# Block sums of w2 made in DRAM scratch, and the seventh block product of the second MLP product made wide

## The chip, the cores and the metric

The kernel runs on one core of one Trainium2 chip. The core has a matrix engine (TensorE, PE in the profile; PEld is its weight load), a vector engine (VectorE, DVE), a scalar engine (ScalarE, ACT), a general engine (GpSimd, POOL), a queue engine (SyncE, SP) and sixteen DMA engines that all queues share. Each engine works through its own instructions in their order, and semaphores tie them together. The metric is the device time of one execution in microseconds; lower is better.

## The reference

One transformer block on `x` of shape (1, 2048, 512), all in float32. First a linear attention, added to `x`:

```python
h = x + A(layernorm(x))
# A: qkv = x @ wqkv, 32 heads of 16
#    phi(q) = [softmax(q w_phi), softmax(-q w_phi)], phi(k) likewise
#    o = phi(q) (phi(k)^T v) / (phi(q) sum(phi(k)) + 1e-6);  A = o @ wo
```

Then an MLP across the 2048 tokens (not the channels), with F = 1792:

```python
g = layernorm(layernorm(h))                       # (S, D)
u = gelu(einsum("sd,sf->df", g, w1) + b1)         # first product,  w1: 2048 x 1792
y = einsum("df,fs->ds", u, w2) + b2               # second product, w2: 1792 x 2048
out = h + y^T
```

## The kernel before

**Precision by parts.** Each float32 matrix is split into a rounded part and a remainder. A product of two such matrices is three matmuls: high by high, high by low, low by high. In the code the first part is made by ACT (a copy into a rounded type) and the second by DVE or POOL (a subtraction), mostly in the helper `split`.

**First stage.** Weights are centred and folded, keys and values are projected for 16 tiles of 128 tokens, and their softmax sums are gathered. PE's order there is written by hand (`PASSES`); the order of the other engines and of SP came from a planner that simulates a timeline.

**Attention stage.** From `ms.enter_context(tc.manual_schedule(...))` on, the order of all five engines is as written. A loop runs `it` over 0 to 17. In iteration `it` SP loads a tile of `x` (`s_x`, the tile `h`), may load a tile pair of w1 for the first part of the first product (`turn`, `fill_load`, `stream`, line 691), and stores the finished `h` of the tile before (`s_h`, line 642). ACT rounds the loaded w1 in the same iteration (`his`, line 677), and DVE later forms its remainder (`flush`, line 684). PE multiplies the numerators (`s_num`), transposes (`s_tr`), does query projections, the output projection `po` (`s_wo`, lines 71 to 73; it needs `oh` from ACT and `ol` from DVE, line 625), and the part of the first product that is already possible (`fill`).

**First and second product.** The rest is a list of 96 steps (`STEPS`): kinds `v u u v v` of the first product, eight steps each, and from step 40 on the second product, eight blocks of 256 output columns (`sp`) with seven steps (`p`) each. In the `u` and `y` steps a 2 x 2 grid of 128-blocks of the weight is multiplied in the manner of Strassen and Winograd with seven block products instead of eight. Each needs one of seven combinations of the four weight blocks and one of seven of the data. The seven weight operands lie in one tile `wraw` of seven places: places 1 to 4 are loaded, and places 0, 5 and 6, and in the second product place 1 as well, are sums. In a `y` step these are four DVE additions, done at once for four steps (`w_sums`, lines 793, 794, 795, 797). In the `u` steps one of the sums is made by an adding DMA of POOL instead (`add_raw`, line 783).

A block product of the second product comes in two shapes. `narrow` (line 951) is three matmuls of 256 columns into one place. `wide` (lines 958 and 960) is one matmul of the rounded weight with the high and low data side by side, 512 columns, and one of 256 columns for the weight's remainder; it fills two places of a bank, and the second has to be added at the end. In the seven full blocks the products P2, P3, P4 and P5 are wide, and P1, P6 and P7 are narrow. The last column block (`last_step`) has all products narrow.

At the end of a column block ACT and DVE read the six banks out and form four output tiles, and POOL adds them to `out` in DRAM with adding DMAs (`store`, line 1001).

**Loads and buffers.** `load_raw(g)` loads the weight of steps 2g and 2g + 1, one transfer of 256 KB each (and one of 64 KB more in `u` steps), into one of two blocks of four steps. It is issued eight steps ahead; SP waits until DVE has read the old contents. `prepare` makes the parts of a step (`w_parts`, lines 66 and 67) two steps ahead in the first product and five in the second.

Of the kernel before, what the change touches and what calls it, by code (L numbers as in the profile page):

```python
# [9 lines left out]
F32 = mybir.dt.float32  # L10
F32R = mybir.dt.float32r
AF = mybir.ActivationFunctionType
ALU = mybir.AluOpType
# [4 lines left out]
P = 128  # L18
# [5 lines left out]
NPR = 2 * NG  # L24
Q_EARLY = 6

PASSES = [(s[0], int(s[1:] or 0)) for s in
          "k5 v f k6 v q k7 q v k8 v q v q k9 k10 v k11 q k12 v k13 v q k14 v".split()]
PKS = 8
SUMS = 8  # L30
Q_TURNS = ((0, 1), (0, 1), (0, 1), (0, 1), (0,), (1,), (0,), (1,))
# [11 lines left out]
def block_kernel(ctx: ExitStack, tc: tile.TileContext, x, xT, wT, phic, wo, w1, b1, w2, b2,  # L43
# [2 lines left out]

    cst = ctx.enter_context(tc.tile_pool(name="cst", bufs=1))
    big = ctx.enter_context(tc.tile_pool(name="big", bufs=NT + 2))

    ident = cst.tile([P, P], F32, name="ident")  # L50
    mask = cst.tile([P, 64], F32, name="mask")
# [55 lines left out]
    X, XH, EQ, PK, VS, SQ, PS, W = {}, {}, {}, {}, {}, {}, {}, {}  # L107

    def load_x(t):
        raw = kk.tile([P, KD, P], F32, name="xraw", bufs=3)  # L110
# [7 lines left out]
    def split_x(t, raw, alone=False):  # L118
# [4 lines left out]
        else:  # L123
            split(X[t][:, 0], X[t][:, 1], raw, nc.gpsimd)

    def stats_x(t):
        junk = kk.tile([P, D], F32, name="sqj", bufs=1)
        st = kk.tile([P, 2], F32, name="st")
        nc.scalar.activation(junk, XH[t], AF.Copy, scale=-1.0 / D, accum_out=st[:, 0:1])
        nc.scalar.activation(junk, XH[t], AF.Square, bias=st[:, 0:1], accum_out=st[:, 1:2])  # L130
        ve = kk.tile([P, 1], F32, name="ve")
        nc.vector.tensor_scalar(ve, st[:, 1:2], 1.0 / D, EPS, op0=ALU.mult, op1=ALU.add)
        nc.gpsimd.tensor_tensor(r1[:, t:t + 1], ve, mhalf[:, :1], op=ALU.pow)

    def proj(t, wh, wl, pool, name, by_part=False, halves=1):
        o = pool.tile([P, D], F32, name=name, tag=name)
# [24 lines left out]
    def logit_ops(src, e, pool):  # L161

        v = src.rearrange("p (j h d) -> p j h d", h=2, d=DH)
        ev = signs(e)
        mx = wk.tile([P, NPR, 2], F32, name="mx")
        mn = wk.tile([P, NPR, 2], F32, name="mn")

        def shift():
            nc.vector.tensor_sub(ev[:, :, 0], v, mx.unsqueeze(3).to_broadcast([P, NPR, 2, DH]))
            if pool:  # L170
                MN.append((ev, mx, mn))
            else:
                nc.vector.tensor_sub(ev[:, :, 1], mn.unsqueeze(3).to_broadcast([P, NPR, 2, DH]), v)  # L173

        return [lambda: nc.vector.tensor_reduce(mx, v, axis=AX.X, op=ALU.max),
                lambda: nc.vector.tensor_reduce(mn, v, axis=AX.X, op=ALU.min),
                shift]

    def negate():

# [9 lines left out]
    def run(*lists):  # L190
        for op in turns(*lists):
            op()

    def exps(t, e):
        nc.scalar.activation(e, e, AF.Exp, scale=r1[:, t:t + 1])  # L195

    def heads(e):
        return e.rearrange("p g (a d) -> p (g a) d", d=DH)

    def k_ops(t, o):  # L200
        PK[t] = kk.tile([P, NG, P], F32, name="pk", bufs=PKS)
        run(logit_ops(o, PK[t], False))

    def k_logits(t):
        k_ops(t, proj(t, wkh, wkl, ps_k, "pk_ps"))
        exps(t, PK[t])

    def v_out(t, o):
        VS[t] = kk.tile([P, D], F32, name="vs", bufs=5)
# [2 lines left out]
    def v_proj(t):  # L212
        v_out(t, proj(t, wvh, wvl, ps_v, "pv"))

    def k_norm(t, z=True):
        sk = wk.tile([P, 2 * H], F32, name="sk", bufs=2)
        nc.vector.reduce_sum(sk, heads(PK[t]), axis=AX.X)
        nc.vector.reciprocal(sk, sk)  # L218
        nc.gpsimd.tensor_mul(heads(PK[t]), heads(PK[t]), sk.unsqueeze(2).to_broadcast([P, 2 * H, DH]))  # L219
        if z and t == 0:  # L220
            nc.gpsimd.tensor_copy(zacc, PK[t])
        elif z:
            nc.gpsimd.tensor_add(zacc, zacc, PK[t])  # L223

    def kv(t):

# [54 lines left out]
    with tc.tile_pool(name="prep", bufs=1) as prep:  # L281
# [77 lines left out]
        with tc.manual_schedule(engines={ET.PE, ET.DVE, ET.Activation, ET.Pool}):  # L359
# [61 lines left out]
            lo_w(0)  # L421
            lo_w(1)
            center(3, False)
        stats_x(3)
        exps(3, PK[3])
        load_h(4)
        stats_x(4)
        k_ops(4, k4)
        exps(4, PK[4])
        v_out(2, v2)  # L430

        def fold_rest():
            for c in range(2, 4):
                fold(c, ps_q, "pu")
                hi_w(c)
                lo_w(c)

        def k_step(t):

            if t + 2 < NT:  # L440
                raw = load_x(t + 2)
                load_h(t + 2)
            if t > 4:
                k_logits(t)
            k_norm(t - 1)
            if t + 2 < NT:
                split_x(t + 2, raw)
                stats_x(t + 2)

        def q_step(_):  # L450
            q_mm()
            run(q_logits(0))
            q_exp(0)
            run(q_sums(0))


        with tc.manual_schedule(engines={ET.PE}):
            k_step(3)
            k_step(4)
            for name, n in PASSES:  # L460
                {"k": k_step, "v": lambda _: v_kv(), "q": q_step, "f": lambda _: fold_rest()}[name](n)

    ms = ExitStack()
    ms.enter_context(tc.manual_schedule(engines={ET.PE, ET.DVE, ET.Activation, ET.Pool, ET.SP}))
# [203 lines left out]
    w1v = w1.rearrange("(k p) f -> p k f", p=P)  # L668
    w2v = w2.rearrange("(k p) s -> p k s", p=P)

    COMING, LATER = [], []

    def his():
# [85 lines left out]
    def load_raw(g):  # L759
        if 2 * g >= len(STEPS):  # L760
            return
        b = g // 2 % 2
        if b not in BLOCK:
            BLOCK[b] = cbb.tile([P, 4, 7, P], F32, name="wraw") if b else wqp.tile([P, 4, 7, P], F32, name="wraw", tag="wq")
        RAW[g] = BLOCK[b][:, g % 2 * 2:g % 2 * 2 + 2]
        for k in range(2):
            src, r, c = blocks(2 * g + k)
# [18 lines left out]
    def w_sums(g):  # L786

        if 2 * g >= len(STEPS) or STEPS[2 * g][0] == "v":
            return
        plain = STEPS[2 * g][0] == "y"  # L790
        raw = BLOCK[g // 2 % 2] if plain else RAW[g]
        if plain:
            nc.vector.tensor_add(raw[:, :, 0], raw[:, :, 3], raw[:, :, 1])
# [35 lines left out]
    for it in range(NT + 2):  # L829
        if it < NT:  # L830
            s_x(it)
        shifted = q["logits"] - len(MN)
        ql = q_logits(0)
        work = turn(it)
# [168 lines left out]
    def wide_step(n, sp, p):  # L1003
        t = 2 * sp
        if p == 0:
            b3, b2 = [new_bank((ps_f, ps_q)[sp % 2]) for _ in range(2)]
            BK[:] = [new_bank(ps_b) for _ in range(4)] + [b3, b2]
        b16, b7, b5, b4, b3, b2 = BK
        first, end = p == 0, p == NP - 1

        def x(m):
            return UB[p, m]

        def ws_(*products):
# [31 lines left out]
        add(e0, l5, u2)  # L1046
# [211 lines left out]
```

## Time and profile before

The median of three runs is 516.4 us (516.31 to 516.42). One execution was profiled:

| what | value |
|---|---|
| the profiled execution's own time | 516.23 us |
| its span, first to last instruction | 514.5 us |
| TensorE clock granted | 1.00 of full speed |
| PE busy | 509.4 us |
| DVE busy | 432.5 us |
| ACT busy | 300.7 us |
| POOL busy | 247.1 us |
| bytes moved by DMA | 61.76 MB |

The span and the time differ by what lies before the first and after the last instruction. The span falls into the first stage (to about 137 us), the attention stage (to about 264 us), the steps of the first product (to about 372 us) and the second product.

How to read the lines. A line of a group gives line, engine, operation, output <- inputs, shapes and count, then busy time and mean length of one in ns, then the idle time of the engine before these instructions and what ended it. A line of the timeline gives start and length in us and then the same. Matmuls are pipelined, so the length of one is longer than the distance between two starts; the distance tells what a matmul costs. A DMA line gives engine that issues, count, KB each and the median time from issue to landing.

### The profile page before, as it was taken

What the parts mean: (1) busy time and instruction counts of PE and PEld (TensorE: products, weight loads), DVE (VectorE), ACT (ScalarE), POOL (GpSimd) and SP (SyncE); (2) the same over time, 40 slices, a digit from 0 to 9 for tenths busy, and PEclk for the clock granted to TensorE, in tenths of its full rate; (3) what the DMA queues carried; (4) which work ended last, traced back from release to release, by engine and by line L of the source; (5) the groups of instructions that cost most, each with busy time, mean ns of one, the idle gap of its engine ahead of it and who ended that gap; (6) DMA issues with size and microseconds to landing.
All of it is one profiled execution on the core that took longest, in us unless ns stands there. A gap on an engine that the chain in (4) does not pass through costs nothing.

```text
span 514.5 us, 10292 instructions
## 1 busy us (share of the span) xinstructions
PE 509.4 (99%) x3954; PEld 439.7 (85%) x3954; DVE 432.5 (84%) x736; ACT 300.7 (58%) x530; POOL 247.1 (48%) x195
## 2 busy tenths in 40 slices
PE   9999999999999999999999999999999999999997
PEld 8888888888877777777788999988899999999997
DVE  6799889989887899699876878986789989968973
ACT  6999853526267878867675636555364434434530
POOL 3579997876999999975203330000002112211220
PEclk9999999999999999999999999999999999999999
DMA  8642301020113233443329784333425687668743
GB/s 306 218 143 84 103 22 42 1 77 8 43 62 103 81 104 126 147 160 126 103 79 256 152 194 120 103 103 102 143 63 126 162 194 172 128 152 192 168 63 71
DMA packets 52112, 61.76 MB, mean 120 GB/s; under 512 B 4704, under 2 KB 38752, under 8 KB 52064
## 3 DMA queue, kind: packets, MB, share of 16 engines
q1 hardware_dynamic: 45440, 52.43, 32.6%
q0 software_dynamic: 6336, 8.52, 12.1%
q8 instruction: 31, 0.51, 0.4%
q10 hardware_dynamic: 288, 0.17, 0.1%
q14 instruction: 17, 0.14, 0.1%
HBM read 49.96 MB, written 11.14 MB: 119 GB/s over the span
## 4 chain that ended last, share of the span: by engine, by line
PE 95%; DVE 2%; ACT 1%; issue 0%; DVEq 0%
PE py L951 22%; PE pu L71 10%; PE pu L72 9%; PE pu L73 9%; PE py L958 9%; PE py L960 4%; PE pk_ps L71 3%; PE pk_ps L72 3%; PE pk_ps L73 3%; PE pv L73 3%; PE pv L72 3%; PE pv L71 3%; PE po L71 3%; PE po L73 2%; PE po L72 2%; PE pn L616 2%
## 5 line engine op out<-in xcount | busy, mean ns | idle before, releaser
L66 ACT ACTIVATE wp<-wraw 128x896 fp32r<-128x896 f32 (+1 forms) x96 | 79.8, 869 | 83.4 <-DVE wraw L797 34.1
L67 DVE TENSOR_TENSOR wp<-wraw,wp 128x896 fp32r<-128x896 f32 (+1 forms) x96 | 92.3, 986 | 20.7 <-ACT wp L66 20.5
L1001 POOL DMA_DIRECT2D out<-u x28 | 24.5, 952 | 170.0 <-ACT u L1047 110.8
L951 PE MATMUL py<-cb,wp 128*128 128x256 f32 x582 | 79.8, 283 | 0.0
L951 PEld LDWEIGHTS py<-cb,wp 128*128 128x128 f32 x582 | 74.0, 191 | 0.0
L490 POOL TENSOR_TENSOR ez<-eq,zB 128x1024 f32<-128x1024 f32 x16 | 38.4, 2404 | 3.8 <-ACT zB L550 3.8
L71 PE MATMUL pu<-hs,wp 128*128 128x512 f32 x96 | 37.4, 389 | 0.0
L72 PE MATMUL pu<-hs,wp 128*128 128x512 f32 x96 | 37.4, 389 | 0.0
L73 PE MATMUL pu<-hs,wp 128*128 128x512 f32 x96 | 37.3, 389 | 0.0
L219 POOL TENSOR_TENSOR pk<-pk,sk 128x1024 f32<-128x1024 f32 x16 | 31.1, 1943 | 11.3 <-DVE sk L218 10.1
L958 PE MATMUL py<-cb,wp 128*128 128x512 f32 x126 | 36.1, 394 | 0.0
L514 POOL TENSOR_TENSOR eq<-eq,w 128x1024 f32<-128x1024 f32 x16 | 32.4, 2026 | 3.5 <-DVE w L511 3.5
L223 POOL TENSOR_TENSOR zacc<-zacc,pk 128x1024 f32<-128x1024 f32 x13 | 31.3, 2406 | 0.5
L783 POOL DMA_DIRECT2D wraw<-in_w x16 | 14.2, 970 | 31.7 <-DMA wraw<-in_w 21.3
L195 ACT ACTIVATE pk<-pk,r 128x1024 f32<-128x1024 f32 x16 | 18.4, 1148 | 15.0 <-DVE pk L173 14.4
L951 PE MATMUL py<-uf,wp 128*128 128x256 f32 x198 | 26.6, 283 | 0.0
L71 PE MATMUL pu<-wq,xs 128*128 128x512 f32 x64 | 26.1, 408 | 0.0
L71 PE MATMUL pu<-hs,whl 128*128 128x512 f32 x64 | 26.0, 406 | 0.0
L71 PE MATMUL po<-woh,oh 128*128 128x512 f32 x64 | 25.3, 395 | 0.1
L72 PE MATMUL pu<-wq,xs 128*128 128x512 f32 x64 | 25.0, 391 | 0.0
L72 PE MATMUL pu<-hs,whl 128*128 128x512 f32 x64 | 25.0, 390 | 0.0
L73 PE MATMUL po<-woh,ol 128*128 128x512 f32 x64 | 25.0, 390 | 0.0
(213 smaller groups left out, 1398.5 us busy)
## 6 DMA issues: line engine op xcount, KB each, us to landing
wraw<-in_w SPq DMA_DIRECT2D x112, 256.0 KB, 3.4
out<-u POOLq DMA_DIRECT2D x21, 256.0 KB, 5.2
xraw<-in_xT SPq DMA_DIRECT2D x16, 256.0 KB, 3.0
xh<-in_x SPq DMA_DIRECT2D x16, 256.0 KB, 2.6
h<-in_x SPq DMA_DIRECT2D x16, 256.0 KB, 2.8
out<-h SPq DMA_DIRECT2D x16, 256.0 KB, 2.0
wraw<-in_wT SPq DMA_DIRECT2D x12, 256.0 KB, 5.2
wraw<-in_w POOLq DMA_DIRECT2D x16, 128.0 KB, 3.9
```

What stands on the lines that cost most here:

```text
L66: nc.scalar.activation(hi, src, AF.Copy)
L67: lo_engine.tensor_sub(lo, src, hi)
L71: nc.tensor.matmul(o, ah, bh, start=first, stop=False)
L72: nc.tensor.matmul(o, ah, bl, start=False, stop=False)
L73: return nc.tensor.matmul(o, al, bh, start=False, stop=last).ins
L219: nc.gpsimd.tensor_mul(heads(PK[t]), heads(PK[t]), sk.unsqueeze(2).to_broadcast([P, 2 * H, DH]))
L223: nc.gpsimd.tensor_add(zacc, zacc, PK[t])
L490: nc.gpsimd.tensor_mul(EZ[t], EQ[t], zB)
L514: nc.gpsimd.tensor_mul(heads(EQ[t]), heads(EQ[t]), W[t].rearrange("p g c h -> p (g c h)").unsqueeze(2).to_broadcast([P, 2 * H, DH]))
L951: nc.tensor.matmul(o, w[:, m[0]], x[:, y], start=opens and i == 0, stop=closes and i == 2, skip_group_check=True)
L958: nc.tensor.matmul(o, wh_[:, m[0]], x(m[1]), start=first, stop=False, skip_group_check=True)
L1001: nc.gpsimd.dma_start(out[t * P:(t + 1) * P, k * HD:], flat(a), accum_op=ALU.add)
```

## The change

1. Scratch in DRAM. For each column block `sp` of w2 a scratch tensor `w2s` of 128 x 7 x 2 x 128 is kept. `copy_w2(sp)` fills it with two DRAM-to-DRAM transfers on SP's queue, in iterations 0 to 7 of the attention loop, directly behind the load of `h`. `add_w2(sp)` adds 128 x 7 x 256 of w2 to it with one adding transfer of POOL's queue; these stand at steps 18, 20, ..., 32 of the first product.
2. Loads. A `y` step now takes places 0 and 1 (both sums) from the scratch and places 2 and 3 to 4 from w2: three transfers instead of one.
3. DVE. The two additions that made places 0 and 1 are gone.
4. P7 is wide in the seven full column blocks. At their end one more ACT copy and one more DVE subtraction bring in the second place of its bank. In a block's first step P7 goes with P5 and P4 instead of before them; in its last step it comes after the narrow products.
5. The order of the first stage is now written out for all engines as a list of tokens (`FIRST`), one token for one operation on one tile.

```diff
+FIRST = """
+X5 H4 X6 a5 X7 b5 a6 b6 H5 X8 X9 s3 a7 S3 b7 a8 H6 X10 u3 b8 l4 r3 s4 m4 n2 k5 S4 o2 H7 X11 x4 y4 s5 N2 v3 u4
...
+    def copy_w2(sp):
+        W2S[sp] = dram.tile([P, NP, 2, P], F32, name=f"w2s{sp}")
+        src = w2v.rearrange("p (j i) s -> p j i s", i=2)
+        for k in range(2):
+            nc.sync.dma_start(W2S[sp][:, :, k], src[:, :, 1 - k, 2 * sp * P:2 * sp * P + P])
+
+    def add_w2(sp):
+        src = w2v.rearrange("p (j i) s -> p j i s", i=2)
+        nc.gpsimd.dma_start(W2S[sp].rearrange("p j k s -> p j (k s)"), src[:, :, 0, 2 * sp * P:2 * sp * P + 2 * P],
+                            accum_op=ALU.add)
...
+        with tc.manual_schedule(engines={ET.PE, ET.DVE, ET.Activation, ET.Pool, ET.SP}):
+            for token in FIRST.split():
+                DO[token[0]](int(token[1:]))
...
+            if kind == "y":
+                nc.sync.dma_start(RAW[g][:, k, 0:2], W2S[i][:, j])
+                nc.sync.dma_start(RAW[g][:, k, 2], src[:, r, c + P:c + 2 * P])
+                nc.sync.dma_start(RAW[g][:, k, 3:5].rearrange("p i s -> p (i s)"), src[:, r + 1, c:c + 2 * P])
+                continue
...
-        if plain:
-            nc.vector.tensor_add(raw[:, :, 0], raw[:, :, 3], raw[:, :, 1])
         nc.vector.tensor_add(raw[:, :, 5], raw[:, :, 0], raw[:, :, 2])
         nc.vector.tensor_add(raw[:, :, 6], raw[:, :, 4], raw[:, :, 5])
-        if plain:
-            nc.vector.tensor_add(raw[:, :, 1], raw[:, :, 1], raw[:, :, 2])
...
         if it < NT:
             s_x(it)
+        if 0 <= it - 0 < 0 + NT // 2:
+            copy_w2(it - 0)
...
-        w3, w2, w5, w4 = (b3, P3), (b2, P2), (b5, P5), (b4, P4)
+        w3, w2, w5, w4, w7 = (b3, P3), (b2, P2), (b5, P5), (b4, P4), (b7, P7)
         if first:
             ws_(w3, w2)
         elif not end:
-            ws_(w3, w2, w5, w4)
+            ws_(w3, w2, w5, w4, w7)
         narrow(b16[:, 0], n, P1, x(1), first, end)
         narrow(b16[:, 1], n, P6, x(5), False, end)
-        narrow(b7[:, 0], n, P7, x(0), first, end)
         if first:
-            ws_(w5, w4)
+            ws_(w7, w5, w4)
         if not end:
             return []
+        ws_(w7)
         ws_(w4, w5)
         ws_(w3, w2)
...
+        nc.scalar.activation(e0, b7[:, 1], AF.Copy)
         sub(u3, u2, b7[:, 0])
...
+        sub(u3, u3, e0)
...
+    for sp, n in ((0, 18), (1, 20), (2, 22), (3, 24), (4, 26), (5, 28), (6, 30), (7, 32)):
+        at(n, add_w2, sp)
```

More of the change, by code (lines that the diff above doesn't have):

```diff
@@ L124, in split_x, with stats_sum, stats_square, stats_var @@
             split(X[t][:, 0], X[t][:, 1], raw, nc.gpsimd)
-    def stats_x(t):
[L127 to L133, printed above, removed]
+    def stats_sum(t):
+        junk = kk.tile([P, D], F32, name="sqj", bufs=1)
+        ST[t] = kk.tile([P, 2], F32, name="st")
+        nc.scalar.activation(junk, XH[t], AF.Copy, scale=-1.0 / D, accum_out=ST[t][:, 0:1])
+    def stats_square(t):
+        junk = kk.tile([P, D], F32, name="sqj", bufs=1)
+        nc.scalar.activation(junk, XH[t], AF.Square, bias=ST[t][:, 0:1], accum_out=ST[t][:, 1:2])
+    def stats_var(t):
+        ST[t], st = kk.tile([P, 1], F32, name="ve"), ST[t]
+        nc.vector.tensor_scalar(ST[t], st[:, 1:2], 1.0 / D, EPS, op0=ALU.mult, op1=ALU.add)
+    def stats_rstd(t):
+        nc.gpsimd.tensor_tensor(r1[:, t:t + 1], ST[t], mhalf[:, :1], op=ALU.pow)
+    def stats_x(t):
+        for f in (stats_sum, stats_square, stats_var, stats_rstd):
+            f(t)
     def proj(t, wh, wl, pool, name, by_part=False, halves=1):
@@ L213, in v_proj, with norm_sum, norm_rec, norm_mul @@
         v_out(t, proj(t, wvh, wvl, ps_v, "pv"))
-    def k_norm(t, z=True):
[L216 to L223, printed above, removed]
+    def norm_sum(t):
+        SK[t] = wk.tile([P, 2 * H], F32, name="sk", bufs=2)
+        nc.vector.reduce_sum(SK[t], heads(PK[t]), axis=AX.X)
+    def norm_rec(t):
+        nc.vector.reciprocal(SK[t], SK[t])
+    def norm_mul(t):
+        nc.gpsimd.tensor_mul(heads(PK[t]), heads(PK[t]), SK[t].unsqueeze(2).to_broadcast([P, 2 * H, DH]))
+    def norm_z(t):
+        if t == 0:
+            nc.gpsimd.tensor_copy(zacc, PK[t])
+        else:
+            nc.gpsimd.tensor_add(zacc, zacc, PK[t])
+    def k_norm(t, z=True):
+        norm_sum(t)
+        norm_rec(t)
+        norm_mul(t)
+        if z:
+            norm_z(t)
     def kv(t):
@@ L423, in block_kernel @@
             center(3, False)
[L424 to L448, printed above, removed]
@@ L450, in q_step, with k_mm @@
-        def q_step(_):
-            q_mm()
[L452 to L461, printed above, removed]
+        LO_K, LO_Q, PV = {4: logit_list(4, k4)}, {}, {2: v2}
+        def k_mm(t):
+            LO_K[t] = logit_list(t, proj(t, wkh, wkl, ps_k, "pk_ps"))
@@ L831, in block_kernel @@
             s_x(it)
+        if 0 <= it < 0 + NT // 2:
+            copy_w2(it - 0)
         shifted = q["logits"] - len(MN)
```

57 lines of the change are left out of this document (44 added, 13 removed).

## The prediction

> **What bounds the kernel now.** I read the page's sums first, then its chain of work, then the busy times by stretch.
>
> ```profile
> span 514.5 us, 10292 instructions
> PE 509.4 (99%) x3954; PEld 439.7 (85%) x3954; DVE 432.5 (84%) x736; ACT 300.7 (58%) x530; POOL 247.1 (48%) x195
> PE 95%; DVE 2%; ACT 1%; issue 0%; DVEq 0%
> 320.00:380.00 60.00, 60.00 (x319) 51.90 (x318) 47.22 (x79) 31.70 (x50) 0.00 (x0) 1.00 0.36 105
> 400.00:480.00 80.00, 80.00 (x553) 74.38 (x552) 69.73 (x105) 35.92 (x57) 15.72 (x18) 1.00 0.76 167
> ```
>
> TensorE (PE) is busy 99% of the span and carries 95% of the chain. The last two rows are stretches of the first and the second product: stretch, length, then busy time of PE, PEld, DVE, ACT, POOL, granted clock, DMA share. PE is busy 60.00 of 60 and 80.00 of 80 at clock 1.00; DVE is at 69.73 of 80, close to full but not the limit. So a saving counts only where it takes PE time away, and any wait put before PE is lost. A busy PE may hide slack, so I check the pitch from starts in the timeline of the second product:
>
> ```profile
> 436.35 1.09 PE L958 MATMUL py<-uf,wp 128*128 128x512 f32 x4
> 437.28 0.63 PE L960 MATMUL py<-uf,wp 128*128 128x256 f32 x4
> 437.75 2.32 PE L951 MATMUL py<-uf,wp 128*128 128x256 f32 x18
> 439.90 0.63 PE L958 MATMUL py<-uf,wp 128*128 128x512 f32 x2
> ```
>
> L958 and L960 are the two matmuls of a wide product: (437.28 - 436.35)/4 = 0.233 us and (437.75 - 437.28)/4 = 0.117 us, 0.350 together. L951 is a third of a narrow product: (439.90 - 437.75)/18 = 0.119 us, 0.358 for three. A narrow and a wide product stream the same 768 columns; the wide one is 0.008 us shorter because it has one matmul fewer.
>
> **The change, part by part.**
>
> *Seventh product wide.* Seven of the eight column blocks have seven steps each: 49 products of 0.358 become 49 of 0.350. Gain on PE: 49 x 0.008 = **0.41 us**. This is all that PE gets out of the edit. The seven extra ACT copies and seven extra DVE subtractions at the ends of the blocks (0.43 us each on DVE, the second row below) are costed at nothing: ACT is busy 35.92 of 80 us, and DVE loses more work than it gains, which is next. If that cover failed it would be at most 7 x 0.43 = 3 us.
>
> ```profile
> L793 DVE TENSOR_TENSOR wraw<-wraw 128x512 f32<-128x512 f32 x14 | 9.6, 687 | 5.8 <-DMA wraw<-in_w 5.2 <-DVE wp L67 0.6
> L1046 DVE TENSOR_TENSOR u<-u 128x256 f32<-128x256 f32 x7 | 3.0, 425 | 0.2
> ```
>
> *Two block sums off DVE.* L793 and its twin L797 go: 14 x 2 x 0.69 = 19 us of DVE. PE never waited for DVE in this stage (80.00 of 80), so the gain on the path is nothing.
>
> *The hand-written order of the first stage.* In the built program PE, DVE, ACT, POOL and SP issue the same instructions in the same order up to the first copy. Cost nothing; a moved wait there would show as PE time before 138 us.
>
> *Sixteen copies on SP's queue.* Each of the first eight attention iterations now issues, behind its load of `h`, two DRAM-to-DRAM copies of 896 runs of 512 B (459 KB each); in iterations 2, 4, 6 and 7 the load of w1 (L691) comes behind both. No copy of this kind is in the trace, so its time is bounded by these rows of the DMA view: the first of 340 to 360 us, the other four of 280 to 300 us (queue: packets, MB, share of 16 engines' time):
>
> ```profile
> q1 hardware_dynamic: 2176, 2.10, 34.5%
> ...
> q1 hardware_dynamic: 2986, 2.34, 41.6%
> q0 software_dynamic: 1090, 0.99, 34.6%
> wraw<-in_w SPq DMA_DIRECT2D x8, 256.0 KB, 3.2
> wraw<-in_w SPq DMA_DIRECT2D x7, 64.0 KB, 3.1
> ```
>
> First row: 0.345 x 16 x 20 = 110 us of engine time for 2.10 MB in 2176 packets, 52.6 us per MB or 51 ns per packet of 1 KB. By bytes a copy takes 0.459 x 52.6 / 16 = 1.51 us on the sixteen engines; if each of its 896 packets cost as much as one of 1 KB, 896 x 51 / 16 = 2.85 us. Between: in the second window q1 spent 0.416 x 320 = 133 us on 8 x 256 packets of 1 KB (104 us at 51 ns) and 7 x 128 of 512 B, so a 512 B packet took (133 - 104)/896 = 33 ns, and a copy takes **1.83 us**. I take that, since the packet size is the same; the ends give the range. A pair holds what is behind it on the queue back by 3.66 us (3.0 to 5.7).
>
> [...]
>
> Now what waits for the load. In each of the four iterations ACT rounds the landed w1 tile (L677), DVE then forms the remainder (L684), and behind it in DVE's fixed order stands L625, whose result PE needs at L73 of `po`. The issue rows of the load, the median landing times from the DMA views around 149, 163, 178 and 186 us, and then ACT, DVE, DVE, PE of each iteration:
>
> ```profile
> 149.24 0.41 SPq L691 DMA_DIRECT2D wraw<-in_w  x1
> 163.01 0.46 SPq L691 DMA_DIRECT2D wraw<-in_w  x1
> 178.20 0.44 SPq L691 DMA_DIRECT2D wraw<-in_w  x1
> 185.79 0.46 SPq L691 DMA_DIRECT2D wraw<-in_w  x1
> ...
> wraw<-in_w SPq DMA_DIRECT2D x1, 256.0 KB, 4.6
> wraw<-in_w SPq DMA_DIRECT2D x1, 256.0 KB, 3.0
> wraw<-in_w SPq DMA_DIRECT2D x1, 256.0 KB, 3.1
> wraw<-in_w SPq DMA_DIRECT2D x1, 256.0 KB, 4.1
> ...
> 153.91 0.62 ACT L677 ACTIVATE whl<-wraw 128x512 fp32r<-128x512 f32 x1
> 155.10 0.83 DVE L684 TENSOR_TENSOR whl<-wraw,whl 128x512 fp32r<-128x512 f32 x1
> 157.14 0.69 DVE L625 TENSOR_TENSOR ol<-pn,oh 128x512 fp32r<-128x512 f32 x1
> 158.94 0.40 PE L73 MATMUL po<-woh,ol 128*128 128x512 f32 x1
> ...
> 169.10 0.61 ACT L677 ACTIVATE whl<-wraw 128x512 fp32r<-128x512 f32 x1
> 170.29 0.85 DVE L684 TENSOR_TENSOR whl<-wraw,whl 128x512 fp32r<-128x512 f32 x1
> 172.33 0.69 DVE L625 TENSOR_TENSOR ol<-pn,oh 128x512 fp32r<-128x512 f32 x1 [0.59 <-ACT oh L620]
> 174.12 0.40 PE L73 MATMUL po<-woh,ol 128*128 128x512 f32 x1
> ...
> 183.94 0.61 ACT L677 ACTIVATE whl<-wraw 128x512 fp32r<-128x512 f32 x1
> 184.81 1.53 DVE L684 TENSOR_TENSOR whl<-wraw,whl 128x512 fp32r<-128x512 f32 x1
> 186.86 0.68 DVE L625 TENSOR_TENSOR ol<-pn,oh 128x512 fp32r<-128x512 f32 x1
> 188.25 0.40 PE L73 MATMUL po<-woh,ol 128*128 128x512 f32 x1
> ...
> 190.40 0.62 ACT L677 ACTIVATE whl<-wraw 128x512 fp32r<-128x512 f32 x1
> 191.36 1.46 DVE L684 TENSOR_TENSOR whl<-wraw,whl 128x512 fp32r<-128x512 f32 x1
> 193.94 0.68 DVE L625 TENSOR_TENSOR ol<-pn,oh 128x512 fp32r<-128x512 f32 x1
> 195.24 0.39 PE L73 MATMUL po<-woh,ol 128*128 128x512 f32 x1
> ```
>
> The margin of a load has three parts: landing to L677, end of L677 to L684, end of L625 to L73.
> - Iteration 2: 153.91 - 153.84 = 0.07; 155.10 - 154.53 = 0.57; 158.94 - 157.83 = 1.11: **1.75 us**.
> - Iteration 4: 3.09 + 0.58 + 1.10: **4.8 us**.
> - Iteration 6: 2.64 + 0.26 + 0.71: **3.6 us**.
> - Iteration 7: 0.51 + 0.34 + 0.62: **1.5 us**.
>
> A delay of 3.66 us overruns these by 1.9, 0, 0.1 and 2.2 us: **PE stalls 4.2 us**. At 3.0 us of delay it is 1.3 + 1.5 = 2.8 us; at 5.7 us it is 4.0 + 0.9 + 2.1 + 4.2 = 11 us. The loads of `h` and the stores behind the copies have an iteration or more in hand: nothing. SP's own issuing (0.4 us per transfer, two more per iteration) lies beside the copies' running and adds nothing to them.
>
> *Eight adding transfers on POOL's queue.* Each is 896 packets of 1 KB. The q0 row gives 0.346 x 320 / 1090 = 102 ns per packet, hence 5.7 us each and 46 us for all. They stand behind the last of the old adding loads and before the first store, when POOL did nothing (0.00 busy between 320 and 380 us) and the DMA engines were 36% busy. The w1 and w2 loads that share the engines are issued eight steps ahead of their use, 8 x 21 x 0.119 = 20 us, so I cost them at nothing. Twice the price (DRAM on both sides is not in the trace) would still finish every block's sum before its own loads; if the cover went, late raw blocks would hold DVE and then PE at about 5.7 us per transfer.
>
> *Three loads per step in place of one.* A step moves 320 KB in 384 packets instead of 256 KB in 256: 128 x (51 + 33 + 51)/16 = 1.08 us of engine time instead of 0.82, per step of 2.5 us (four wide and three narrow products). DMA share rises from 0.76 to about 0.86. The L793 row shows DVE already waiting 5.2 us in all for these loads; two adds fewer per block of four steps (1.4 us) pay for later landings of that size. Cost nothing, at worst rival C.
>
> **The sum.** The profiled execution has span 514.5 us and time 516.23 us, 0.17 under the median of 516.4. 516.4 - 0.4 + 4.2 = **520.2 us**.
>
> **Rivals.**
> - A, hidden: the copies pass without holding the loads so long. It decides below a delay of about 1.8 us a pair, where the stalls of iterations 2 and 7 (0.05 + 0.3) equal the gain. For it: the loads in iterations 2 and 7 landed slowly (4.6 and 4.1 us against 3.0), and if whatever slowed them were absent both margins grow by over a us. Against it: 0.92 MB in 1.8 us is above any rate in the quoted rows. Time 516.0.
> - B, the other side, faster by more than 1 us: the second product is in truth paced by DVE or by weight loads, so that 19 us less DVE work, or 49 weight loads fewer, shorten it. It needs PE starts that are uneven; a pitch of 0.119 over 18 matmuls and PE 80.00 of 80 speak against it. If every step gained one weight load's visible time, 49 x 0.117 = 5.7 us, the time would be near 511, or 515 with the copies' stall; only a fraction is thinkable.
> - C, a new wait in the second product: the last of twelve loads of a four-step block lands later, DVE's in-order queue stands at the next sum, and the read-out of finished banks behind it holds PE. At 1 us for each of seven block ends, 7 us more: 527 with the stall above. Against it: DVE has 1.4 us more room per block.
>
> **How the numbers follow.** Forecast (stall of 2 to 8 us in attention) 0.55; A 0.27; C or a copy as dear as the upper bound 0.12; B 0.06. About 0.2% (1 us) is what a measurement of this kernel can tell from no change. A falls mostly within it: faster 0.06, same 0.27, slower 0.67. The forecast alone spans 518.8 to 524 by the two ends below 2.4 us a copy; with A taken in, the range is 515.8 to 524.0, which leaves out B and C.
>
> **What would show it.** Right: in the changed profile the load of w1 (L691 before) lands 3 to 4 us later in iterations 2 and 7, ACT shows idle time before the rounding of `whl` released by DMA, PE has gaps before `po` between 155 and 200 us of some 2 us each, and the second product's step is 0.008 us shorter with no gaps. Wrong: no such gaps (A), PE gaps after 385 us (C), or a second product shorter by more than 0.5 us (B). The likeliest error is the copies' price: 0.5 us per copy moves the sum by 2 us.

## The result, and the profile after

The changed kernel takes 533.0 us (median of five, 531.7 to 537.4) against 516.4 us before: 1.035 times the time, interval 1.030 to 1.040. The profiled execution has a span of 531.3 us and a time of 533.0 us.

The page of the changed kernel: span, busy times, and the chain of work by engine.

```profile
span 531.3 us, 10418 instructions
PE 516.0 (97%) x3905; PEld 440.7 (83%) x3905; DVE 421.3 (79%) x715; ACT 301.8 (57%) x537; POOL 258.3 (49%) x203
PE 77%; DMA 8%; DVE 7%; ACT 5%; SPq 2%; issue 1%; DVEq 0%; ACTq 0%
```

PE carried 95% of the chain before; now DMA, DVE and ACT have 20% of it. PE stands twice. Matched instruction by instruction against the trace of before, PE's starts are late by 0.56 us from 8 us on, by 9.36 us where the first product begins (273.11 us), still by 9.36 at step 40 (381.45 us), by 16.84 us from step 48 (408.70 us) to the end. So the attention stage lost 8.8 us and the first steps of the second product 7.5 us; beyond the 0.56 us of the start nothing else lost anything.

Attention, iteration 2, from the timeline of the changed kernel (start, length, then engine and line as in the prediction; L68 are the copies, L733 the load, L719 to L96 what was L677 to L71):

```profile
149.73 1.67 SPq L68 DMA_DIRECT2D w2s<-in_w  x2
151.50 0.70 SPq L733 DMA_DIRECT2D wraw<-in_w  x1
...
157.22 1.95 POOL L559 TENSOR_TENSOR eq<-eq,w 128x1024 f32<-128x1024 f32 x1
157.33 0.63 ACT L719 ACTIVATE whl<-wraw 128x512 fp32r<-128x512 f32 x1 [2.79 <-DMA wraw<-in_w]
157.99 1.72 DVE L726 TENSOR_TENSOR whl<-wraw,whl 128x512 fp32r<-128x512 f32 x1 [2.27 <-ACT whl L719]
...
160.83 0.67 DVE L670 TENSOR_TENSOR ol<-pn,oh 128x512 fp32r<-128x512 f32 x1
...
161.56 0.51 PE L96 MATMUL po<-woh,oh 128*128 128x512 f32 x1 [2.39 <-DVE ol L670]
```

This is the chain of the prediction: ACT waits for the load behind the two copies, DVE for ACT, PE for DVE. From start to start the gap of PE is 2.56 us (the bracket counts from a modelled end). Iterations 4, 6 and 7 have gaps of 0.38, 1.21 and 1.98 us. Two things are new. DVE's subtraction took 1.72 us where it took 0.83, beside a multiplication of POOL; and 3.41 us of half clock follow the gap (below).

The adds, on the page of the changed kernel (a group, then a DMA issue line), and the DMA view of 360 to 380 us:

```profile
L72 POOL DMA_DIRECT2D w2s<-in_w x8 | 11.9, 1490 | 77.2 <-issue 77.2
...
w2s<-in_w POOLq DMA_DIRECT2D x8, 896.0 KB, 11.5
```

```profile
q0 software_dynamic: 1801, 1.82, 70.7%
q1 hardware_dynamic: 2151, 1.62, 29.0%
...
wraw<-w2s SPq DMA_DIRECT2D x6, 128.0 KB, 7.2
wraw<-in_w SPq DMA_DIRECT2D x5, 128.0 KB, 7.1
wraw<-in_w SPq DMA_DIRECT2D x6, 64.0 KB, 6.9
```

An add takes 11.5 us from issue to landing, and POOL's next transfer starts 11.1 to 12.8 us after it, 0.6 to 0.9 us behind its last packet: 77.2 us of idle time in the first row. The first starts at 322.7 us and the last lands at 417.5: 95 us, not 46. In 360 to 380 us the adds take 70.7% of the DMA engines, all of which are busy, and a load of a `y` step lands after 7 us. (q0 is the queue of POOL, q1 that of SP.) What waits for those loads, in the timeline at step 44:

```profile
390.65 0.69 DVE L840 TENSOR_TENSOR wraw<-wraw 128x512 f32<-128x512 f32 x1 [12.18 <-DMA wraw<-in_w]
...
393.54 0.73 PE L1004 MATMUL py<-cb,wp 128*128 128x512 f32 x2 [2.07 <-ACT wp L91]
```

DVE's sum of a four-step block waits 12.18 us for the last of its loads, the parts behind it come late, and PE stands. That load was late twice over. SP also stood before issuing, for earlier loads of its own to land; its waits from 376 to 392 us have this row (total, times, longest):

```profile
SPq L814 <- DMA wraw<-w2s: 4.6, 2, 2.9
```

Counted from the first matmul of step 40, the load was issued 3.9 us later than in the last version below, and it took 7.4 us to land instead of 2.7.

### The profile page after: what moved, and what is told of

Read it like the earlier page. It is cut to its first block, busy times and chain, and to the rows that moved or that the text cites. A ratio compares the mean times of both kernels' runs of the same rounds, so it can differ in the third digit from the quotient of the medians.

```text
span 531.3 us, 10418 instructions
## 1 busy us (share of the span) xinstructions
PE 516.0 (97%) x3905; PEld 440.7 (83%) x3905; DVE 421.3 (79%) x715; ACT 301.8 (57%) x537; POOL 258.3 (49%) x203
## 4 chain that ended last, share of the span: by engine, by line
PE 77%; DMA 8%; DVE 7%; ACT 5%; SPq 2%; issue 1%; DVEq 0%; ACTq 0%
PE py L997 17%; PE py L1004 9%; DMA wraw<-in_w 7%; PE pu L96 7%; PE pu L97 6%; PE pu L98 6%; PE py L1006 5%; PE pk_ps L96 3%; PE pk_ps L97 3%; PE pk_ps L98 3%; PE pv L96 3%; PE pv L97 3%; PE pv L98 3%; PE po L96 2%; PE po L98 2%; PE po L97 2%
## 5 line engine op out<-in xcount | busy, mean ns | idle before, releaser
L997 PE MATMUL py<-cb,wp 128*128 128x256 f32 x477 | 66.6, 284 | 0.7 <-DVE u L1086 0.7
L997 PEld LDWEIGHTS py<-cb,wp 128*128 128x128 f32 x477 | 61.4, 193 | 0.9 <-DVE u L1086 0.9
L72 POOL DMA_DIRECT2D w2s<-in_w x8 | 11.9, 1490 | 77.2 <-issue 77.2
L1004 PE MATMUL py<-cb,wp 128*128 128x512 f32 x161 | 46.0, 398 | 2.5 <-ACT wp L91 2.1
L96 PE MATMUL pu<-hs,wp 128*128 128x512 f32 x96 | 37.4, 389 | 0.0
L259 POOL TENSOR_TENSOR pk<-pk,sk 128x1024 f32<-128x1024 f32 x16 | 31.0, 1943 | 11.2 <-DVE sk L256 10.1
L840 DVE TENSOR_TENSOR wraw<-wraw 128x512 f32<-128x512 f32 (+1 forms) x22 | 13.0, 591 | 26.1 <-DMA wraw<-in_w 23.4
L1004 PEld LDWEIGHTS py<-cb,wp 128*128 128x128 f32 x161 | 27.7, 190 | 6.5 <-ACT wp L91 2.3
L96 PE MATMUL po<-woh,oh 128*128 128x512 f32 x64 | 26.5, 414 | 5.8 <-DVE ol L670 5.8
L726 DVE TENSOR_TENSOR whl<-wraw,whl 128x512 fp32r<-128x512 f32 x16 | 23.4, 1463 | 9.1 <-ACT whl L719 9.1
L1006 PEld LDWEIGHTS py<-cb,wp 128*128 128x128 f32 x161 | 25.8, 192 | 3.7
L1006 PE MATMUL py<-cb,wp 128*128 128x256 f32 x161 | 27.4, 284 | 0.0
## 6 DMA issues: line engine op xcount, KB each, us to landing
w2s<-in_w POOLq DMA_DIRECT2D x8, 896.0 KB, 11.5
```

The source lines that it names most:

```text
L96: nc.tensor.matmul(o, ah, bh, start=first, stop=False)
L259: nc.gpsimd.tensor_mul(heads(PK[t]), heads(PK[t]), SK[t].unsqueeze(2).to_broadcast([P, 2 * H, DH]))
L997: nc.tensor.matmul(o, w[:, m[0]], x[:, y], start=opens and i == 0, stop=closes and i == 2, skip_group_check=True)
L1004: nc.tensor.matmul(o, wh_[:, m[0]], x(m[1]), start=first, stop=False, skip_group_check=True)
L1006: nc.tensor.matmul(o[:, 0], wl_[:, m[0]], x(m[1])[:, 0], start=False, stop=last, skip_group_check=True)
```

## The experiments

Every time beside a ratio is a median over several executions; the others are one execution. The kernel before had medians of 516.4 to 517.1 us beside them. One execution can differ from another by up to 1.2 us by its start alone: the clock first became full at 3.94 us in the trace of before and between 3.94 and 7.2 us in the others (7.19 us made all of PE's work 1.16 us late).

### Which part costs what

**The copies behind the load of w1.**

```diff
-        if 0 <= it < 0 + NT // 2:
-            copy_w2(it - 0)
...
         work = turn(it)
+        if 0 <= it < 0 + NT // 2:
+            copy_w2(it - 0)
```

> Compared with the changed kernel, the two copies of an iteration stand behind its load of w1 instead of ahead of it. Theory (order on the queue): what PE lost in the attention stage, 8.8 us of the 16.8, came from the w1 load landing behind the copies, so it goes: about 524 us, no PE gap over 0.5 us between 155 and 210 us, and no stretch of half clock there. Rival (the copies crowd engines and memory, wherever they stand): the gaps stay, 530 us or more. The stall near 390 us stays in both.

Measured: 522.8 us. PE's lateness is 1.16 us at 8 us and 1.15 us at the start of the first product: attention loses nothing. The gap at step 44 is still there, with its half clock. The order on the queue is the whole loss of the attention stage.

**No adds.**

```diff
-    for sp, n in ((0, 18), (1, 20), (2, 22), (3, 24), (4, 26), (5, 28), (6, 30), (7, 32)):
-        at(n, add_w2, sp)
```

> The changed kernel without the eight adding transfers (the two block sums then lack one term each, so the output is not the reference's). Theory (the adding transfers take half of the DMA engines until 417 us, and the first loads of the second product come late): the 7.5 us lost between 390 and 410 us go, about 525.5 us. Rival (three loads per step in place of one are what is late): the loss stays, about 533 us.

Measured: 524.3 us, lateness 8.05 us at the start of the first product and 8.01 at the end. The adds are the whole loss of the second product; the three loads per step cost nothing without them.

**The copies alone.** The kernel before with `copy_w2` at its place and nothing else.

> The kernel before, with the sixteen copies added in the same places and nothing else. Theory: the whole loss of the attention stage and nothing more, 516.4 + 8.8 = about 525 us, with one stretch of half clock of 3.4 us behind the first long PE gap. Rival (part of the attention loss comes from the first stage's written order or from the rest of the change): clearly less, 520 us or under.

Measured: 523.5 us; gaps of 2.53, 1.51 and 1.58 us in iterations 2, 6 and 7, none in iteration 4. No half clock, where the theory had one stretch of it, though the first gap is as long as that of the changed kernel.

**P7 wide alone**, with its extra copy and subtraction, the sums left on DVE.

> The kernel before, with the seventh product wide and its extra ACT copy and DVE subtraction, and with the four DVE sums kept; no scratch. Theory (PE alone counts): 49 products 0.008 to 0.010 us shorter, 516.0 us (0.4 to 0.5 less than before). Rival (DVE, at 87% of the second product, has no room for seven more subtractions): same or slower, 516.4 to 518 us.

Measured: 517.3 us, ratio 1.0017 (1.0007 to 1.0027). The first expectation missed, the rival held: from the first `py` matmul, which stands in the `u` steps of the first product, to the last column block took 205.30 us instead of 204.96, and all of the difference lies in the seven full column blocks (121.44 instead of 121.10). Without the sums taken off DVE the wide product costs 0.3 us.

**No adds, copies behind the load.** The two edits above together.

> The changed kernel with the copies behind the load of w1 and without the eight adds (the two sums then lack one of their two terms). What is left of the change is the copies, three loads per step, the two DVE sums gone and the wide P7. Theory: neither stage loses anything, and the wide product gains 0.04 us as in the run without adds: 516.4 us, 516.0 to 516.8. Rival: the gain of 0.41 us is there and was covered: 516.0 or below, with the seven blocks 0.4 us shorter than before. Rival: three loads per step cost time when the stage starts earlier: 517.5 or more.

Measured: 516.7 us, ratio 0.9999 (0.999 to 1.0008). Level, as the first expectation had it; the gain of 0.41 us is not there.

### The adds: how they hurt

**Adds beside single loads.** The kernel before with the copies behind the load of w1 and the eight adds at their places; its loads stay one transfer per step.

> The kernel before with all copies (behind the load of w1) and all eight adds of the change at their places, while the steps still load one transfer of 256 KB and form all sums on DVE (the scratch is not read). Theory: the stall of the second product needs both, the adds and the dearer loads: a step's loads take 0.33 of the engines instead of 0.43 beside the adds' 0.55 to 0.7, so most of it goes: 516.4 to 518.4 us. Rival: the adds alone make every load late and PE stands after 385 us for 3 us or more: 519.5 to 522.

Measured: 518.4 us, at the upper edge of the first expectation; PE loses 2.2 us in the seven column blocks. The expectation that "most of it goes" was too high: with the changed kernel's loads and the copies behind them (the first experiment) the same stretch lost 5.2 us, 1.7 of them half clock, so the adds alone make 2.2 of 3.5 us. The rest comes with the three loads per step, or with the other DVE sums and the wide P7, in which the two kernels also differ; no run separates these. SP's waits speak for the loads: between 364 and 395 us it stood for landings of its own loads for 4.5 us in the first experiment, and never here or without the adds.

**Four adds early, in attention.**

```diff
+        if it in (11, 13, 15, 17):
+            add_w2((it - 11) // 2)
...
-    for sp, n in ((0, 18), (1, 20), (2, 22), (3, 24), (4, 26), (5, 28), (6, 30), (7, 32)):
+    for sp, n in ((4, 18), (5, 20), (6, 22), (7, 24)):
```

> The changed kernel with the copies behind the load of w1, four of the adds in attention iterations 11, 13, 15 and 17, and four at steps 18 to 24, so that the last should land before 372 us. Theory: the adds cost time only where they run beside the loads of the second product: no stall there, 516.4 us (516.0 to 517.5). Rival: in attention they make the loads of h and w1 late in their turn, with PE gaps between 225 and 275 us: 518 or more. Rival: the three loads and the late sums hold DVE at step 44 whatever the adds do: 520 or more.

Measured: 533.3 us, ratio 1.032 (1.029 to 1.034). The second product no longer stands (204.91 us from the first `py` matmul to the last column block), as expected; but the first rival came true far above its size. From the timeline of PE, and the groups of 225 to 280 us:

```profile
272.15 0.49 PE L96 MATMUL pu<-hs,whl 128*128 128x512 f32 x1 [2.26 <-ACT whl L719]
274.68 0.79 PE L97 MATMUL pu<-hs,whl 128*128 128x512 f32 x1 [2.04 <-DVE hs L711]
```

```profile
L719 ACT ACTIVATE whl<-wraw 128x512 fp32r<-128x512 f32 x6 | 3.8, 626 | 15.7 <-DMA wraw<-in_w 15.6
```

Loads of w1 beside an add landed after 5.6 to 10.1 us instead of 2.8 to 4.7; ACT waited 15.6 us for six of them, and PE, with three windows of half clock, lost 15 us. The last four adds, at 328 to 376 us, cost nothing.

### Why the gap is 2.55 us

**One pair, in iteration 2 only**, then **one copy, in iteration 2 only** (the kernel before with `copy_w2` under `if it == 2`, the second time with `range(1)` for `range(2)`).

> The kernel before with one pair of copies, in iteration 2 only (the scratch is not read). Theory: the pair on its own holds back the load behind it, so PE stands about 2.5 us before the first po matmul of iteration 2, as it did with all sixteen copies (2.53 us), and nowhere else: 519.0 us, and 520.7 if the clock halves afterwards. [...] Rival: the copies of iterations 0 and 1 were still being worked off and made the load late; then the stall is below 1 us and the time below 517.5. [...]

Measured: 519.7 us, gap 2.55 us, no half clock. The copies of earlier iterations have no part in it.

> The kernel before with one copy, half a pair, in iteration 2 (the scratch is not read). Theory: the load behind it waits for the bytes in front of it, so its lateness is about half of the pair's 2.8 us, 1.4 to 1.7 us. The margin to the first po matmul is 1.75 - 0.47 = 1.28 us, and DVE loses up to 0.9 us if its operation then falls beside one of POOL's: PE stands 0.1 to 1.3 us, no half clock: 516.6 to 518 us. Rival: any copy ahead of the load costs the whole stall of 2.5 us, whatever its size (519 us).

Measured: 520.5 us, gap 2.55 us, and half clock after it: the rival, against the theory. Half the bytes, the same gap. The timeline of the run with one copy shows why:

```profile
156.77 1.94 POOL L525 TENSOR_TENSOR eq<-eq,w 128x1024 f32<-128x1024 f32 x1
156.93 2.33 DVE L695 TENSOR_TENSOR whl<-wraw,whl 128x512 fp32r<-128x512 f32 x1 [1.66 <-ACT whl L688]
...
161.11 0.50 PE L82 MATMUL po<-woh,oh 128*128 128x512 f32 x1 [2.38 <-DVE ol L636]
```

DVE's subtraction starts 0.16 us behind POOL's multiplication and ends at 159.26, 0.55 us after POOL's end at 158.71. In the changed kernel it starts 0.77 us behind and also ends 0.55 us after. The same holds in the runs with the copies alone, with one pair, and with a pair and tile 3 cut short (below): in the five traces the subtraction starts 0.16 to 0.84 us into POOL's 1.94 us and ends 0.54 to 0.55 us after them, and the gap is 2.53 to 2.56 us.

**POOL's multiplication cut short.** First of the tile before, by mistake:

```diff
     def s_pq(t):
-        nc.gpsimd.tensor_mul(heads(EQ[t]), heads(EQ[t]), W[t].rearrange("p g c h -> p (g c h)").unsqueeze(2).to_broadcast([P, 2 * H, DH]))
+        n = 1 if t == 3 else 2 * H
+        nc.gpsimd.tensor_mul(heads(EQ[t])[:, :n], heads(EQ[t])[:, :n],
+                             W[t].rearrange("p g c h -> p (g c h)")[:, :n].unsqueeze(2).to_broadcast([P, n, DH]))
```

> One copy in iteration 2 as before, but POOL's multiplication of the numerators of tile 3 (1.94 us, in which DVE's late subtraction fell) is done for 1 of its 32 heads only, so that tile's output is left unscaled. Theory: the 2.55 us with one copy were 0.9 us of late load and 1.65 us of DVE waiting until 0.55 us after the end of POOL's operation; the subtraction then takes 0.7 us in place of 2.33 and PE stands 0.9 us (0.7 to 1.2), with no half clock: 517.4 to 518 us. Rival: DVE is slowed by the landing transfers or the late load itself sets the 2.55 us: the gap stays at 2.3 to 2.6 us.

> The pair of copies in iteration 2, with POOL's multiplication of tile 3 cut to 1 of 32 heads in the same way. Theory: the pair's load is 0.35 us later than the single copy's, and DVE's subtraction no longer waits (1.88 us becomes 0.7): PE stands 1.35 us (1.1 to 1.6), so without POOL the gap does grow with the bytes in front. Rival: it stays at 2.3 to 2.6 us.

Measured: 516.8 us without a gap, and 520.6 us with one of 2.55 us. Neither tests the theory, since the operation at 157 us was still there, 1.94 us long. With one copy the load came early this time (SP issued the copy in 0.67 us, in the run above in 2.1), and DVE's subtraction started at 156.09 us, ahead of POOL's operation at 157.75. So one copy gave no gap or the whole one; why SP's issue took longer in one run than in the other is not known.

Then with `t == 4`, the right tile:

> The pair of copies in iteration 2, with POOL's multiplication of tile 4 done for 1 of its 32 heads only (that tile's output is left unscaled). In the two runs before, the multiplication of tile 3 was cut, which comes one iteration too early: the 1.94 us operation at 157 us, beside which DVE's subtraction falls, was still there. Theory: without it the subtraction takes 0.7 us in place of 1.65 to 1.88, and PE stands 1.5 us (1.0 to 1.8) in place of 2.55, with no half clock: 518 to 518.8 us. Rival: the gap stays at 2.5 to 2.6 us, so something else ends it.

Measured: 517.7 us, gap 1.25 us:

```profile
156.89 0.22 POOL L526 TENSOR_TENSOR eq<-eq,w 128x16 f32<-128x16 f32 x1
157.38 0.69 DVE L697 TENSOR_TENSOR whl<-wraw,whl 128x512 fp32r<-128x512 f32 x1 [1.98 <-ACT whl L690]
...
159.93 0.50 PE L82 MATMUL po<-woh,oh 128*128 128x512 f32 x1 [1.08 <-DVE ol L638]
```

Without POOL's long operation the subtraction takes 0.69 us, and the gap halves. The late load makes some 1.25 us of it, the wait for POOL 1.3.

### Is it the change, or its places?

The whole change, computed in full, with copies and adds moved to where no load is due soon. Four versions follow. In each, late adds stand at step 18 and after, copies 4 to 7 (3 to 7 in the third) behind the load of w1, the first copies behind the loads of tiles 12 and 13 of `x`.

> The whole change, computed in full, with every copy and add moved to where no load is due soon: copies 0 to 3 behind the last but two loads of the first stage (from about 66 us), copies 4 to 7 behind the load of w1 in iterations 4 to 7, adds 0 to 2 ahead of POOL's multiplications of tiles 7, 9 and 12 and add 3 ahead of its first ez (about 83 to 138 us), adds 4 to 7 at steps 18 to 24. Theory: price and place are the whole loss, so it goes: 516.7 us like the run without adds (516.2 to 517.5), no PE gap over 0.5 us. Rival: the adds hold POOL or the loads of wo and h in the first stage as they held the loads of w1 in attention: 519 or more, with PE gaps before 145 us. If the change had a gain of its own it would show here: below 516.0.

Measured: 521.0 us, ratio 1.0066 (1.0044 to 1.0088). The theory missed by one add, on POOL and DVE of that timeline:

```profile
74.67 1.67 POOL L72 DMA_DIRECT2D w2s<-in_w  x1 [6.17 <-DMA w2s<-in_w]
...
78.86 0.15 DVE L162 TENSOR_SCALAR ve<-st 128x1 f32<-128x1 f32 x1 [7.04 <-POOL r L165]
```

It stood ahead of its copy's landing and held POOL for 6.17 us, DVE behind POOL, and PE by 2.6 us and a half-clock window.

> As the version with all copies and adds in quiet places, but adds 0, 1 and 2 ahead of POOL's multiplications of tiles 9, 11 and 13 (about 91, 102 and 114 us). There add 0 stood at 68 us on POOL and waited 6.17 us for its copy, DVE behind POOL 7.04 us, and PE lost 2.4 us and then 1.7 at half clock; the adds after it cost nothing. Theory: by 91 us the copies have landed, so nothing waits: 516.7 us (516.2 to 517.5), no PE gap over 0.5 us, and the whole change, computed in full, stands level with the kernel before. Rival: an add at any place of the first stage holds DVE behind POOL or the loads of wo: 518.5 or more.

Measured: 522.1 us, ratio 1.011 (1.009 to 1.013). Now an add issued at 107.0 us ran beside the four loads of `wo`, which landed after 7.6 to 8.0 us; PE stood 1.0 and 1.2 us at 125 us, and ran 3.41 us at half clock. The other adds cost nothing, early or late. The four executions took 520.2 to 523.0 us, the traced one 520.2; what the others lost beyond it is not known.

> The whole change, computed in full: copies 0 to 2 in the first stage behind the load of tile 13, copies 3 to 7 behind the load of w1 in iterations 3 to 7, adds 0 and 1 ahead of POOL's multiplications of tiles 9 and 11 (about 82 and 97 us, where adds cost nothing in the run before), add 2 behind that of tile 15 (about 121 us, after the four loads of wo at 111 to 113 us, which add 2 made land after 7.6 to 8.0 us in place of 2.8 to 3.9 in that run, and PE stood 2.2 us at 125 us for them), adds 3 to 7 at steps 18 to 26, so that the last should land by 371 us, before the loads for step 44 are issued. Theory: no PE gap over 0.5 us, 516.8 us (516.2 to 517.5). Rival: a fifth add behind the four reaches into the second product and PE stands 1 us or more at step 44: 518 or more.

Measured: 520.2 us, ratio 1.0065 (1.0048 to 1.0082): the rival. The first stage lost nothing, but the fifth late add landed at 372.9 us, and PE stood at step 44 (1.48, 0.74, 0.90 and 0.58 us).

> The whole change, computed in full: copy 0 behind the load of tile 12 of x, copies 1 to 3 behind that of tile 13, copies 4 to 7 behind the load of w1 in iterations 4 to 7; adds 0, 1 and 2 ahead of POOL's multiplications of tiles 8, 10 and 12 (about 74, 90 and 102 us), add 3 behind that of tile 15 (121 us), adds 4 to 7 at steps 18 to 24, so that the last lands by 361 us. In the run before, three early adds cost nothing and the stall came from the fifth late one, which landed at 372.9 us. Theory: no PE gap over 0.5 us anywhere, 516.8 us (516.2 to 517.5): the whole loss was one of places. Rival: add 0 beside the copies holds POOL, DVE and PE at 84 us, or add 2 the loads of wo: 518.5 or more. If the change had a gain of its own, it would be below 516.0.

Measured: 517.1 us (eleven executions), ratio 1.0008 (0.9998 to 1.0017). Its page:

```profile
span 514.5 us, 10425 instructions
PE 509.3 (99%) x3905; PEld 437.6 (85%) x3905; DVE 417.5 (81%) x715; ACT 303.1 (59%) x537; POOL 258.7 (50%) x203
PE 95%; DVE 2%; ACT 1%; DMA 1%; issue 0%; POOL 0%; DVEq 0%
```

The span and the chain are those of before. Adds run at 74 to 131 us and 313 to 360 us, and no gap of PE that the kernel before does not have is left. So the loss of 16.6 us lay in the places of copies and adds (no run separates whether an add holds up the loads beside it at the engines or at the memory behind them), and a well placed version neither gains nor loses: none of these kernels beats the one before.

## Why the prediction was wrong

The sign was right and the first mechanism too; the time was 12.8 us short and outside the range. Nor was the likeliest error that it named, the price of the copies, the one that occurred.

- **Seventh product wide, gain 0.41 us: not there.** The seven blocks take 121.05 us in the last version against 121.10. Summed from each start to the next, their narrow matmuls fell by 17.43 us in all and their wide ones rose by 17.38. P7 itself fell from 17.64 to 17.16 us, more than forecast, but the other six products rose by 0.43: P6, which now ends the run of narrow matmuls as P7 did, takes 17.62 instead of 17.45. The step that failed took the pitch inside a run of equal matmuls and left the neighbours as they were.
- **Block sums off DVE, no gain on the path: right.** The cover named for the extra subtractions is there: with the sums left on DVE the wide product costs 0.3 us, with them gone nothing.
- **First stage written out, nothing: right.** The lateness is 0.56 us from 8 us on, which goes with the later first full clock (5.26 us instead of 3.94), and does not grow before the first `po` gap.
- **Copies, 3.66 us a pair: right in size.** A packet of 512 B took 31 to 32 ns in the pairs of iterations 2, 4, 6 and 7, against 33. With PE's lateness taken off, the changed kernel's loads landed 2.9, 4.9, 4.1 and 3.7 us later than before in iterations 2, 4, 6 and 7. In iteration 2 the copies landed at 154.6 and 156.6 us and the load behind them at 157.3. Whether SP's own issuing "adds nothing" stays open: the two issues took 1.67 us there and put the load's own issue 1.7 us later, but the load still landed right behind the second copy.
- **PE stalls 4.2 us: the term was mis-sized, 8.8 us measured.** The margins added a landing, a fixed 0.83 us of DVE and a wait for L73. But where DVE's operation fell beside one of POOL's it lasted until 0.55 us after that one's end (the quoted 1.53 and 1.46 us of iterations 6 and 7 showed it varies), PE needs `ol` in order at the first of the three matmuls (158.47 us in the trace of before, where the prediction took 158.94), 0.47 us earlier, and 1.7 us are half clock, which the sum did not have at all. The rest is the gaps of 2.56, 0.38, 1.21 and 1.98 us in iterations 2, 4, 6 and 7, where 1.9, 0, 0.1 and 2.2 were forecast, and about 1 us in small steps.
- **Adds, 46 us and nothing: the step that failed most.** The price per packet held up, though it came from adds that land in SBUF (first row, kernel before, 280 to 300 us); between two tensors in DRAM (second row, changed kernel, 322.7 to 417.5 us) a packet took 0.570 x 16 x 94.8 / 7296 = 119 ns against 102, or 6.6 us for an add's 896 packets if it had all sixteen engines.

```profile
wraw<-in_w POOLq DMA_DIRECT2D x6, 128.0 KB, 3.5
...
q0 software_dynamic: 7296, 7.34, 57.0%
q1 hardware_dynamic: 12388, 10.18, 37.2%
```

What failed is the overlap. The 46 us took the engines undivided and the adds back to back; but the loads beside them took 37.2%, an add landed after 11.5 us, and POOL issued the next only then, so the eight ran for 95 us, into the second product. And the loads beside them were costed at nothing. "Twice the price would still finish every block's sum before its own loads" looked at the sums, but it was the other loads that came late. This is rival C by its place (DVE's in-order queue at a late sum). Its size fits by luck: 7.5 us were lost, 1.7 of them half clock, where C had 7, but at one place, the second block of four steps, and because of the adds, not at seven block ends.

- **Three loads per step, nothing: right without the adds**; beside them up to 1.3 us, by the difference above.

Rival A fell with the first gap, rival B with the 121.05 us.

## What to carry to other kernels

Price a bulk transfer not by its own time alone but by the loads that are due while it runs: here sixteen copies cost the attention stage 8.8 us ahead of the loads of w1 and nothing behind them, and eight adds cost the second product 7.5 us at their first places and nothing in the last version. So look, stage by stage, for which load has the least margin, and put the transfer behind that load on its queue and away from it in time. Where a late operand enters another engine's in-order queue, look at what a third engine does beside it: of the gap of 2.55 us, 1.3 us were a wait for one operation of POOL. And a change of which every part is hidden at its best gains nothing: in the last version DVE has 15 us less to do (417.5 for 432.5 us) at a ratio of 1.0008; only PE's own pitch, summed over real sequences, could have paid here.

## What the runs showed of the hardware

**DVE waited for POOL.** In all traces, a `whl` subtraction of DVE that started beside a running POOL tensor operation, more than 0.2 us before its end, ended 0.54 to 0.56 us after that end, in all of 195 cases (21 of them in the traces of before and of the changed kernel): 2.33 us long in one run, 1.72 in another, 0.69 with POOL idle. So it lasted 0.55 us beyond POOL's end, 0.14 us less than the 0.69 us that it takes alone. In all of these cases POOL had started first; nothing here is measured for the other order.

**Half clock started on a grid of 3.413 us.** The stretches of full clock that a half-clock stretch ended were 81.92, 122.88, 157.01, 249.17 and 385.71 us long from their first full clock: 24, 36, 46, 73 and 113 times 3.413 us. So these starts lie on one grid, counted from the first full clock. Windows on that grid in the changed kernel, then in the run with the copies alone (stretch, length, busy PE, PEld, DVE, ACT, POOL, granted clock, DMA share, GB/s):

```profile
158.86:162.27 3.41, 1.02 (x5) 0.62 (x4) 3.41 (x6) 3.35 (x8) 3.26 (x3) 1.00 0.86 239
162.27:165.68 3.41, 3.41 (x10) 2.62 (x9) 2.21 (x6) 1.11 (x2) 2.29 (x4) 0.50 0.04 12
199.81:203.22 3.41, 1.64 (x8) 1.04 (x6) 2.50 (x5) 3.10 (x8) 1.73 (x3) 1.00 0.74 234
203.22:206.63 3.41, 3.36 (x15) 2.79 (x16) 3.34 (x6) 3.34 (x7) 2.14 (x2) 1.00 0.02 5
```

```profile
156.62:160.03 3.41, 2.85 (x55) 1.99 (x54) 1.86 (x2) 2.45 (x7) 3.37 (x3) 1.00 0.88 258
160.03:163.44 3.41, 1.59 (x7) 1.32 (x8) 3.41 (x5) 3.35 (x6) 2.71 (x2) 1.00 0.65 174
163.44:166.85 3.41, 3.41 (x17) 2.80 (x16) 2.57 (x9) 1.27 (x5) 3.09 (x4) 1.00 0.10 39
```

The same gap of 2.5 us lies within one window in the first trace and across a border in the second; only the first is followed by a window at 0.50, which costs 1.7 us, half of its 3.41. Over all runs, windows at full clock with 0.5 to 1.34 us of busy PE were followed by half clock and windows with 1.83 us or more were not; between, 1.59 and 1.64 were not, 1.66 and 1.75 were, which is closer than the modelled ends of matmuls can decide. One window that was itself at half clock, with 2.10 us busy, was followed by another (four adds early, 273.37 us). The length of the gap alone did not decide: of 2.53 and 2.55 us there was no half clock after it with the copies alone and with the pair in iteration 2, and of 2.55 and 2.56 us there was with one copy and in the changed kernel.
